# An attention and expert kernel with its first two experts' token lists cut in two parts each, six routing batches, and the routing of the last chunk put ahead

## The chip, the cores and the metric

One core of one Trainium2 chip runs the whole program. The metric is the device time of one execution in microseconds (us), taken as the median of several runs. A profiled execution gives the trace that the rows below come from.

## The reference

A decayed linear attention for 4 batches of 768 tokens with 8 heads of 64 features, and behind it a mixture of 16 experts (4 groups of 4), in which each of the 3072 tokens goes to one expert.

```python
for t in range(S):                      # attention, S = 768
    state = gamma * state + outer(k[:, :, t], v[:, :, t])
    y[:, :, t] = scale * (q[:, :, t] @ state)
x = y.transpose(0, 2, 1, 3).reshape(B * S, H * D)      # 3072 x 512
g_idx = argmax(x @ w_group, axis=1)                    # group, weight g_w by softmax
e_idx = argmax(xg @ w_expert[g], axis=1)               # expert in it, weight e_w by softmax
h = maximum(xg[mask_e] @ w1[g, e], 0)                  # 512 -> 1024
out[tok_idx] = (g_w * e_w)[:, None] * (h @ w2[g, e])   # 1024 -> 512
```

The inputs drawn with the reference's own seed give experts 0 and 1 (group 0) 210 and 200 tokens. Of expert 0's, 92 lie in the first 12 chunks of 128 tokens and 118 in the last 12; of expert 1's, 94 and 106.

## The kernel before, in words

**Attention** runs over 24 chunks of 128 tokens, six to a batch. For one chunk `attention` issues the products with the state (L262), with the scores of two chunks ago (L275), the new state (L238), a product that brings the logits of the chunk before into token order (L318), two groups of transposes (L195, L293), the scores of the chunk after next (L216) and the logits of this chunk (L307). VectorE multiplies the output by its decays (`xt`, L287) and masks the scores (`pf`, L223). All products that belong to routing write one PSUM tile, `log`.

**Routing** goes by batches of chunks (`BATCHES`). `route` is a generator of VectorE steps, one to a `yield`: logits to a one-hot matrix `oh`, the ranks of the tokens by a few small products of `oh` (L368, L370) into `log`, the softmax weights, then `r1` and `nb` (L397, L399), which read the ranks, and the token's slot (L419). `route_steps` draws a few steps at three places of each chunk. After the ranks' products it pauses for three calls. `enlist` then scatters each chunk's token numbers and weights into the experts' lists in DRAM (`meta`, L427, an indirect DMA that GpSimd issues), `listed` reads a list back (`mt`, L614, on SP's queue), `gather` fetches its tokens' rows (`xg`, L624, GpSimd), and `xtrans` transposes them and splits them into a 16-bit high and low part (L642 to L645).

**Experts.** Weights come as 1 MB loads (`wload`, L576; four to an expert, four buffers). `wsplit` cuts 512 or 1024 columns at a time into a high part on ScalarE (L601) and the rest on VectorE or GpSimd (L602). `layers` runs one tile of tokens: 96 products of the tile's width for the first layer (L665), ScalarE and VectorE making `hh` and `hl` from it (L670, L671), and a second layer of 24 products 512 wide (L689), or of 96 products of the tile's width where the tile has at most 116 tokens (L713, with transposes at L773). `scatter` writes the result (L792).

Experts 0 and 1 are done first, in tiles of their own, so that they can begin before the routing ends: `ua` (expert 0, up to 128 tokens of the first 12 chunks), `ub` (78 of the next 7), `uc` (59 of the rest), `va` (expert 1, 128 of the first 12 chunks), `vb` (128 of the rest). `order` then sorts the other 14 experts by their counts; `us[0]` to `us[13]` are run in that order with widths from 256 down to 173, each with the next one's loads and splits under it. Tokens that exceed a tile's width are left to a loop at the end (`general`).

The order on each engine is the order of the code: the schedule is manual, and each engine takes its instructions strictly in turn. Behind the last chunk the code emits, in this order: the rest of `ua`'s layers mixed with the last route, the scatters into the lists, the reads of `ub`'s list, `va`'s layers with the splits of `va`'s weights and the steps of `order` under them, `ub`, `uc`, `vb`, and `us[0]`. The loads of `us[0]`'s weights stand on GpSimd's queue, behind the gathers of `uc` and `vb`.

Of the kernel before, what the change touches and what calls it, by code (L numbers as in the profile page):

```python
# [13 lines left out]
U32 = mybir.dt.uint32  # L14
# [8 lines left out]
P = 128  # L23
# [36 lines left out]
BATCHES = [(0, 4), (4, 4), (8, 4), (12, 7), (19, 5)]  # L60
# [34 lines left out]
class Kernel:  # L95
    def __init__(self, tc, qk, vb, wr, w1p, w2p, cst, dec, out):
# [8 lines left out]
        self.pause = 0  # L105
# [220 lines left out]
    def route(self, i):  # L326
# [67 lines left out]

        rkv = rk.rearrange("p (c x) -> p c x", x=NX)
# [7 lines left out]
        V.tensor_tensor(r2, r1, oh[:, 0:n, :], ALU.mult)  # L403
        yield 1
# [10 lines left out]
        sf = t("sf")  # L415
        V.tensor_reduce(sf, r2, axis=AX.X, op=ALU.add)
        yield 1
        slot = rp.tile([P, BM], U32, name="slot", bufs=3)[:, 0:n]
        V.tensor_copy(slot, sf)  # L419
        yield 1  # L420
        self.todo += [(slot, src, c) for c in range(n)]

    def enlist(self, slot, src, c):
# [9 lines left out]
        if self.done > MIDDLE:  # L433
            tc.declare_no_dep(i.ins, group="middle", reason="no later token enters this list")
            tc.add_to_no_dep_group("middle", i.ins)
# [168 lines left out]
    def listed(self, u, group=None):  # L604
# [42 lines left out]
    def layers(self, u):  # L647
# [6 lines left out]
        for f2 in range(4):  # L654
# [16 lines left out]
            nc.vector.scalar_tensor_tensor(hl[:, f, 0:W], hv[:, :, 0:W], 0.0, hh[:, f, 0:W], ALU.max, ALU.subtract)  # L671
# [177 lines left out]
    def attention(self, extra, beside):  # L849
# [20 lines left out]
        for ch in range(NCH):  # L870
# [4 lines left out]
            steps = 4 if late else 5  # L875
# [14 lines left out]
            self.route_steps(steps)  # L890
# [262 lines left out]
```

## Time and profile before

| what | us |
|---|---|
| median of 3 runs (467.91 to 469.46) | 468.16 |
| the profiled execution | 468.46 |
| its span, from the first to the last instruction | 466.6 |
| PE busy in the span | 430.1 (92%) |
| DVE, ACT, POOL busy | 296.3, 235.1, 178.7 |

PE is TensorE's matmuls, PEld its weight loads, DVE VectorE, ACT ScalarE, POOL GpSimd, SPq and POOLq the queues on which DMAs are issued. An idle time stands in square brackets with what ended it. Starts of matmuls are true, while a busy time includes the pipeline's depth, so that steps are best taken from start to start. PEclk is the granted clock, 1.00 for 2.4 GHz.

### The profile page before, as it was taken

How to read it: one execution, taken by the hardware profiler on the slowest of the kernel's cores; microseconds unless marked ns; L12 is line 12 of the kernel's file. 1: busy time of each engine (PE TensorE's matmuls, PEld its weight loads, DVE VectorE, ACT ScalarE, POOL GpSimd, SP SyncE). 2: the span in 40 equal slices, each digit the busy share in tenths (PEclk: the TensorE clock that was granted, in tenths of full speed). 3: DMA queues.
4: the chain of work that ended last, by engine and by line, in shares of the span. 5: the costliest groups of instructions: out<-in, count | busy, mean ns of one | idle time of the engine just before them, and what ended most of it. 6: DMA issues, size and time to landing. Idle time of an engine off the chain costs nothing.

```text
span 466.6 us, 13547 instructions
## 1 busy us (share of the span) xinstructions
PE 430.1 (92%) x5679; PEld 348.5 (75%) x5679; DVE 296.3 (64%) x490; ACT 235.1 (50%) x398; POOL 178.7 (38%) x148
## 2 busy tenths in 40 slices
PE   7997989899789687799999999999999999999991
PEld 3886868788676287485878879788788788788770
DVE  2448476566549321867768897587777777787720
ACT  1333435444454033745556556665576676676610
POOL 3624557570585553210323335054153153142011
PEclk9999899999999798999999999999999999999997
DMA  7979797796560274676768687787977887987000
GB/s 244 353 235 313 233 266 229 254 287 208 179 222 2 53 295 181 217 256 235 247 211 243 244 251 256 275 269 270 291 263 271 305 274 271 325 278 286 11 29 30
DMA packets 36024, 106.86 MB, mean 229 GB/s; under 512 B 14687, under 2 KB 15327, under 8 KB 28283
## 3 DMA queue, kind: packets, MB, share of 16 engines
q1 hardware_dynamic: 24059, 88.65, 56.9%
q0 software_dynamic: 11904, 17.34, 10.7%
q8 instruction: 45, 0.74, 0.6%
q14 instruction: 16, 0.13, 0.1%
HBM read 93.55 MB, written 13.81 MB: 230 GB/s over the span
## 4 chain that ended last, share of the span: by engine, by line
PE 67%; issue 18%; POOL 6%; DVE 3%; DMA 2%; ACT 1%; SPq 1%; POOLq 0%; ACTq 0%
PE hps L665 21%; PE yps L739 8%; PE yps L689 7%; PE yps L741 5%; PE op L275 5%; PE sc L216 5%; PE op L262 2%; POOL out L792 2%; PE stp L238 2%; PE tpx L642 2%; PE tp L293 2%; PE kt L195 2%; PE log L307 2%; POOL meta L427 2%; POOL xg L624 1%
## 5 line engine op out<-in xcount | busy, mean ns | idle before, releaser
L602 DVE TENSOR_TENSOR wl<-wf,wh 128x1024 bf16<-128x1024 f32 (+1 forms) x121 | 144.6, 1204 | 39.8 <-ACT wh L601 39.6
L665 PE MATMUL hps<-xbl,wh 128*128 128x128 bf16 (+16 forms) x608 | 136.8, 243 | 2.9 <-DVE xbl L645 1.6
L665 PE MATMUL hps<-xbh,wh 128*128 128x128 f16 (+16 forms) x608 | 136.9, 243 | 2.2 <-ACT xbh L644 2.2
L665 PE MATMUL hps<-xbh,wl 128*128 128x128 f16 (+16 forms) x608 | 136.8, 243 | 0.0
L601 ACT ACTIVATE wh<-wf 128x1024 f16<-128x1024 f32 (+1 forms) x136 | 134.2, 999 | 0.1
L792 POOL DMA_INDIRECT out<-yo,mt x33 | 43.0, 1303 | 194.9 <-ACT yo L757 173.5
L665 PEld LDWEIGHTS <-wh 128*128 128x128 f16 x1216 | 105.2, 99 | 5.9 <-issue 3.3
L624 POOL DMA_INDIRECT xg<-xd,mt x33 | 53.3, 1614 | 26.7 <-DMA mt<-meta 13.3
L670 ACT ACTIVATE hh<-hps 128x256 f16<-128x256 f32 (+16 forms) x76 | 35.8, 472 | 54.4 <-PE hps L665 54.1
L665 PEld LDWEIGHTS <-wl 128*128 128x128 bf16 x608 | 59.7, 99 | 4.2 <-issue 3.3
L671 DVE SCALAR_TENSOR_TENSOR hl<-hps,hh 128x256 bf16<-128x256 f32 (+16 forms) x76 | 40.0, 528 | 35.9 <-ACT hh L670 35.5
L741 PEld LDWEIGHTS <-wh 128*128 128x128 f16 x704 | 44.7, 98 | 21.0
L223 DVE TENSOR_TENSOR pf<-sc,cst 128x512 f32<-128x512 f32 x48 | 30.9, 685 | 36.1 <-PE sc L216 36.1
L644 ACT ACTIVATE xbh<-tpx 128x512 f16<-128x512 f32 (+15 forms) x33 | 17.1, 517 | 49.9 <-PE tpx L642 49.8
L645 DVE TENSOR_TENSOR xbl<-tpx,xbh 128x512 bf16<-128x512 f32 (+15 forms) x33 | 19.4, 589 | 22.7 <-ACT xbh L644 22.6
L602 POOL TENSOR_TENSOR wl<-wf,wh 128x512 bf16<-128x512 f32 (+1 forms) x15 | 20.3, 1355 | 34.7 <-ACT wh L601 32.8
L739 PE MATMUL yps<-wh,hh 128*128 128x512 f16 x88 | 33.4, 380 | 0.0
L739 PE MATMUL yps<-wh,hl 128*128 128x512 f16 x88 | 33.4, 379 | 0.0
L739 PE MATMUL yps<-wl,hh 128*128 128x512 bf16 x88 | 33.4, 379 | 0.0
L427 POOL DMA_INDIRECT meta<-src,slot x24 | 27.4, 1140 | 9.5 <-issue 5.3
L741 PEld LDWEIGHTS <-wl 128*128 128x128 bf16 x352 | 23.1, 98 | 10.4
L216 PE MATMUL sc<-ld 64*128 64x128 f32 x384 | 28.4, 288 | 2.2 <-DMA ld<-qk 2.2
(138 smaller groups left out, 682.3 us busy)
## 6 DMA issues: line engine op xcount, KB each, us to landing
wf<-w1p SPq DMA_DIRECT2D x28, 1024.0 KB, 7.8
wf<-w2p SPq DMA_DIRECT2D x28, 1024.0 KB, 7.2
ld<-qk SPq DMA_DIRECT2D x23, 512.0 KB, 7.0
xd<-xr SPq DMA_DIRECT2D x24, 256.0 KB, 3.5
vt<-vb SPq DMA_DIRECT2D x6, 768.0 KB, 8.1
wf<-w1p SPq DMA_DIRECT2D x8, 256.0 KB, 4.3
wf<-w2p SPq DMA_DIRECT2D x8, 256.0 KB, 4.1
wf<-w1p POOLq DMA_DIRECT2D x2, 1024.0 KB, 7.0
```

The lines of the kernel that those rows point to most:

```text
L216: nc.tensor.matmul(s["sc", par][:, cs], kT[rs, cs], qT[rs, cs], start=True, stop=True)
L427: i = nc.gpsimd.indirect_dma_start(out=self.metaf, out_offset=bass.IndirectOffsetOnAxis(ap=slot[:, c:c + 1], axis=0), in_=src[:, c, :], in ...
L601: nc.scalar.activation(u["wh"][i][:, cs], u["wf"][i][:, cs], AF.Copy)
L602: (eng or nc.vector).tensor_tensor(u["wl"][i][:, cs], u["wf"][i][:, cs], u["wh"][i][:, cs], ALU.subtract)
L624: nc.gpsimd.indirect_dma_start(out=xg[0:r, i, :], out_offset=None, in_=self.xd[0:n, :], in_offset=bass.IndirectOffsetOnAxis(ap=mt[0:r, i, ...
L665: nc.tensor.matmul(hv[:, a, 0:W], l[:, k, fs], r[:, k, 0:W], start=(n == 0), stop=(n == 11))
L670: nc.scalar.activation(hh[:, f, 0:W], hv[:, :, 0:W], AF.Relu)
L671: nc.vector.scalar_tensor_tensor(hl[:, f, 0:W], hv[:, :, 0:W], 0.0, hh[:, f, 0:W], ALU.max, ALU.subtract)
L689: nc.tensor.matmul(ps[0:r, :], l[:, k, ts], m[k], start=(n == 0), stop=(n == 23))
L739: nc.tensor.matmul(big, h[:, k, 0:P], w[k], start=(n == 0), stop=(n == 23))
L741: nc.tensor.matmul(yv[:, d, 0:r], w[k][:, d * P:d * P + P], h[:, k, P:P + r], start=(n == 0 and d == 0), stop=(n == 23), skip_group_check= ...
L792: s = nc.gpsimd.indirect_dma_start(out=self.out, out_offset=bass.IndirectOffsetOnAxis(ap=mt[0:r, i, 0:1].bitcast(U32), axis=0), in_=yo[0:r ...
```

## The change

Expert 0 gets two tiles, `ua` and `ub`, both 128 wide, in place of 128, 78 and 59; `uc` is gone, and both experts' second tiles take all tokens after the 12th chunk. The batches of the route become 4, 4, 4, 5, 4 and 3 chunks. Within a batch the softmax weights come first and the ranks' products after them, with `r1` and `nb` right behind these, and only at the first place of a chunk. Six of expert 1's eight splits now stand in chunks 20 to 22 (two did before); the last four quarter splits of `ua` move from VectorE to GpSimd. Expert 1's loads come one in each of chunks 18 to 21. Behind the last chunk the route of the last batch is emitted at once, `hl` of the layers that run meanwhile is held back until its slots are made, and `order`, the loads of `us[0]` (now on SP's queue) and all gathers come ahead of `va`. The splits and loads of `us[0]` and `us[1]` begin under `ub` and `vb`.

```diff
-EARLY, MIDDLE = (12, 19)
-PARTS = [
-    [(EARLY, 128, 0), (MIDDLE, 78, NX), (NCH, 59, NX + 1)],
-    [(EARLY, 128, 1), (NCH, 128, NX + 2)],
-]
+EARLY = 12
+PARTS = [[(EARLY, P, e), (NCH, P, NX + e)] for e in range(2)]
...
-BATCHES = [(0, 4), (4, 4), (8, 4), (12, 7), (19, 5)]
+BATCHES = [(0, 4), (4, 4), (8, 4), (12, 5), (17, 4), (21, 3)]
...
                 if 4 <= ch <= 19:
-                    self.wsplit(ua, ch - 4, 16, nc.gpsimd if ch < 16 else nc.vector)
-                if ch in (18, 21, 22, 23):
-                    self.wload(va, (18, 21, 22, 23).index(ch))
-                if ch in (21, 22):
-                    self.wsplit(va, ch - 21, eng=nc.gpsimd)
+                    self.wsplit(ua, ch - 4, 16, nc.gpsimd)
+                if 18 <= ch <= 21:
+                    self.wload(va, ch - 18)
+                if ch in (20, 21):
+                    self.wsplit(va, 2 * ch - 40)
+                    self.wsplit(va, 2 * ch - 39, eng=nc.gpsimd)
...
                 if ch == NCH - 2:
+                    self.wsplit(va, 4)
+                    self.wsplit(va, 5)
                     self.first = self.layers(ua)
...
-                if ch == 20 and place == 1:
+                if ch == 19 and place == 1:
...
-            first(2)
+            first(1)
             self.logits(last)
+            assert not self.steps
+            route = self.route(len(BATCHES) - 1)
+            while next(route) != "wait":
+                pass
+            self.held = []
+            first(1)
             self.trans_mm(last)
             self.x_store(last)
             first(2)
...
+            for _ in route:
+                pass
             while self.todo:
                 self.enlist(*self.todo.pop(0))
-            self.gather(ub)
...
+            self.listed(ub)
+            self.listed(vb)
...
+            self.steps.append(self.order())
+            self.route_steps(99)
...
+            self.wsplit(va, 6)
+            self.wsplit(va, 7)
+            self.picked(us[0], 0)
+            self.listed(us[0])
+            for i in range(4):
+                self.wload(us[0], i)
...
-            self.picked(us[0], 0, (ET.SP, ET.Pool))
-            for i in range(4):
-                self.wload(us[0], i, nc.gpsimd)
...
-            for k in self.layers(uc):
...
```

The first place is PE in a chunk of the attention at whose start a batch's ranks are made (before, then after); `log` is the routing tile, and the last product of each piece writes it.

```order
L238 MATMUL stp<-vs,kk 64x64 x7
L368 LDWEIGHTS stri
L368 MATMUL log<-oh,stri 128x80 [waits Activation_49]
...
L370 MATMUL log<-oh,ones 128x16
L318 MATMUL log<-cst,ls 128x20
L293 MATMUL tp<-ident,xt 128x128 [waits PE_49]
...
L307 MATMUL log<-xt,wr 32x128 [waits DVE_49,Activation_49]
```

```order
L236 MATMUL stp<-vs,kk 64x64 x7
L387 LDWEIGHTS stri
L387 MATMUL log<-oh,stri 128x80 [waits Activation_49]
...
L389 MATMUL log<-oh,ones 128x16
L316 MATMUL log<-cst,ls 128x20 [waits DVE_49]
L291 MATMUL tp<-ident,xt 128x128 [waits PE_49]
...
L305 MATMUL log<-xt,wr 32x128 [waits Activation_49]
```

The wait on VectorE has moved from the last product of the chunk to the one right behind the ranks.

The second place is POOL from the last chunk's vector product on: before, five scatters into the lists behind a split, `ub`'s gather, a result, two gathers and the loads of `us[0]`; then after.

```order
L602 TENSOR_TENSOR wl<-wf,wh 128x1024 [waits DMAHW3_49,DMAHW0_49,DMAHW4_49,PE_49,Activation_49]
L427 DMA meta<-src,slot 60800x2 [waits DMASW6_49,DVE_49]
...
L427 DMA meta<-src,slot 60800x2 [waits DMASW2_49]
L624 DMA xg_80<-xd,mt 78x512 [waits DMAHW4_49,DMAHW6_49,DMAHW3_49,DMAHW7_49,DMAHW1_49,DMASW3_49]
L792 DMA out<-yo,mt 3072x512 [waits DMASW4_49,Activation_49]
L624 DMA xg_80<-xd,mt 59x512 [waits DMAHW4_49,DMAHW3_49,DMAHW5_49,DMAHW1_49,DMAHW7_49,DMASW5_49,PE_49]
...
L580 TENSOR_LOAD ord [waits DVE_49]
L576 ISA
L576 DMA wf<-w1p 128x2048 [waits DMASW0_49,Pool_49]
```

```order
L425 DMA meta<-src,slot 57600x2 [waits DMASW4_49,DVE_49]
...
L425 DMA meta<-src,slot 57600x2 [waits DMASW7_49]
L425 DMA meta<-src,slot 57600x2 [waits DMASW0_49,DVE_49]
L425 DMA meta<-src,slot 57600x2 [waits DMASW1_49]
L425 DMA meta<-src,slot 57600x2 [waits DMASW2_49]
L795 DMA out<-yo,mt 3072x512 [waits DMASW3_49,Activation_49]
L623 DMA xg_80<-xd,mt 128x512 [waits DMAHW5_49,DMAHW4_49,DMAHW6_49,DMAHW3_49,DMAHW7_49,DMAHW1_49,DMASW4_49]
L623 DMA xg_80<-xd,mt 128x512 [waits DMAHW7_49,DMASW5_49,PE_49]
```

Four scatters (of the batch of chunks 17 to 20) and three (of the last) now stand there, then `ua`'s result and the gathers; the loads are no longer on this queue.

The third place is VectorE behind the last batch's ranks, before and after.

```order
L419 CAST slot<-sf 128x5 [waits DVE_49]
L1034 MEMSET xg_2314 128x1024 [waits DMAHW3_49,DMAHW2_49,DMAHW6_49,DMAHW1_49,Pool_49]
L602 TENSOR_TENSOR wl<-wf,wh 128x1024 [waits DMAHW3_49,DMAHW5_49,DMAHW2_49,DMAHW6_49,DMAHW0_49,Activation_49]
...
L671 SCALAR_TENSOR_TENSOR hl<-hps,hh 128x2x128 [waits Activation_49] x3
...
L457 TENSOR_TENSOR gt<-key 1x256 [waits DVE_49]
...
L645 TENSOR_TENSOR xbl<-tpx,xbh 128x4x78 [waits Activation_49]
L476 CAST ord<-ordf 1x16 [waits DVE_49]
```

```order
L407 CAST slot<-sf 128x3 [waits DVE_49]
...
L1022 SCALAR_TENSOR_TENSOR hl<-hps,hh 128x2x128 [waits Activation_49] x2
L672 SCALAR_TENSOR_TENSOR hl<-hps,hh 128x2x128 [waits Activation_49]
L644 TENSOR_TENSOR xbl<-tpx,xbh 128x4x128 [waits Activation_49]
...
L475 CAST ord<-ordf 1x16 [waits DVE_49]
...
L601 TENSOR_TENSOR wl<-wf,wh 128x1024 [waits DMAHW2_49,Activation_49]
L601 TENSOR_TENSOR wl<-wf,wh 128x1024 [waits Activation_49]
```

The held `hl` come behind the slots, then `order`, and only two splits of expert 1 are left, behind `order`.

## Rows read from the trace of the kernel before

**Rows 1.** The profile page's first line.
```profile
span 466.6 us, 13547 instructions
```

**Rows 2.** Busy time by stretch of the span: us, then PE, PEld, DVE, ACT and POOL busy (with the number of instructions), granted clock, share of the DMA engines' time, GB/s.
```profile
140.00:150.00 10.00, 9.17 (x116) 7.04 (x116) 9.45 (x27) 4.40 (x7) 5.14 (x4) 1.00 0.02 2
150.00:160.00 10.00, 5.87 (x30) 2.82 (x28) 5.54 (x13) 0.82 (x2) 6.94 (x5) 0.80 0.12 35
170.00:180.00 10.00, 6.28 (x194) 6.07 (x191) 1.82 (x5) 2.78 (x7) 3.54 (x4) 1.00 0.99 391
230.00:250.00 20.00, 20.00 (x148) 15.06 (x146) 14.35 (x23) 11.13 (x15) 6.39 (x4) 1.00 0.71 240
```

**Rows 3.** What PE waited for in the first 135 us: us in total, times, longest.
```profile
PE log L307 <- DVE nb L399: 7.9, 4, 2.4
```

**Rows 4.** The timeline of chunks 6 to 8, PE and VectorE: start, us, engine, line, tile, shape, idle before.
```profile
45.28 0.43 PE L307 MATMUL log<-xt,wr 128*32 128x128 f32 x8 [2.43 <-DVE nb L399]
51.65 0.43 PE L307 MATMUL log<-xt,wr 128*32 128x128 f32 x8
52.01 0.67 PE L262 MATMUL op<-ld,V 64*64 64x128 f32 x16
53.31 0.86 DVE L287 TENSOR_TENSOR xt<-op,gx 128x256 f32<-128x256 f32 x2 [0.27 <-PE op L275]
54.09 0.40 PE L318 MATMUL log<-cst,ls 128*128 128x20 f32 x2
56.43 0.42 PE L307 MATMUL log<-xt,wr 128*32 128x128 f32 x8
```

**Rows 5.** The timeline in the last chunks: `ua`'s list and tokens, the start of chunks 22 and 23 (L262), and the start of `va` (the first 128-wide product at 144.89).
```profile
115.71 0.87 SPq L614 DMA_DIRECT2D mt<-meta  x2
118.33 1.09 POOL L624 DMA_INDIRECT xg<-xd,mt  x1 [13.33 <-DMA mt<-meta]
123.01 0.67 PE L262 MATMUL op<-ld,V 64*64 64x128 f32 x16
125.81 0.60 PE L642 MATMUL tpx<-ident,xg 128*128 128x128 f32 x4
129.30 0.67 PE L262 MATMUL op<-ld,V 64*64 64x128 f32 x16
144.89 0.22 PE L665 MATMUL hps<-xbh,wh 128*128 128x128 f16 x1
```

**Rows 6.** The timeline of the last route: VectorE's steps, the split on POOL beside one of them, and PE's wait for `oh`.
```profile
137.06 2.85 DVE L352 SCALAR_TENSOR_TENSOR q<-d,cst 128x100 f32<-128x100 f32 x1
137.63 2.15 POOL L602 TENSOR_TENSOR wl<-wf,wh 128x1024 bf16<-128x1024 f32 x1
140.83 0.20 PE L368 MATMUL log<-oh,stri 128*128 128x96 bf16 x1 [2.15 <-DVE oh L361]
143.50 0.17 DVE L419 CAST slot<-sf 128x5 uint32<-128x5 f32 x1
```

**Rows 7.** The timeline of the scatters into the lists on POOL (the fourth and fifth of five), the gather behind them, and SP's next reads of the lists.
```profile
149.36 2.58 POOL L427 DMA_INDIRECT meta<-src,slot  x1 [0.31 <-issue]
152.24 1.17 POOL L427 DMA_INDIRECT meta<-src,slot  x1 [0.30 <-issue]
153.71 1.08 POOL L624 DMA_INDIRECT xg<-xd,mt  x1 [0.30 <-issue]
154.58 10.80 SPq L614 DMA_DIRECT2D mt<-meta  x8
```

**Rows 8.** The chain of work that ended last, from the gather of `ub`'s tokens to `us[1]`: start, us, what. "issue" is time in which the engine waited for nothing that the profile shows.
```profile
157.14 0.78 PE tpx L642 x4
157.92 5.09 PE yps L689 x12
163.01 3.36 PE hps L665 x96
...
172.24 1.32 issue
...
177.59 2.98 issue
...
181.38 2.33 PE hps L665 x24
...
184.15 4.02 PE hps L665 x72
188.17 2.59 PE yps L689 x12
190.76 0.44 PE tpx L642 x4
...
197.37 11.99 PE hps L665 x95
...
220.56 10.08 PE hps L665 x96
```

**Rows 9.** Groups of instructions by line and shape: count, busy us, mean ns of one, idle before.
```profile
L601 ACT ACTIVATE wh<-wf 128x1024 f16<-128x1024 f32 x120 | 124.3, 1049 | 0.0
L602 POOL TENSOR_TENSOR wl<-wf,wh 128x1024 bf16<-128x1024 f32 x3 | 6.4, 2150 | 2.7 <-ACT wh L601 2.7
```

**Rows 10.** The page's DMA issues: count, KB of one, us from issue to landing.
```profile
wf<-w1p SPq DMA_DIRECT2D x28, 1024.0 KB, 7.8
```

More of the change, by code (lines that the diff above doesn't have):

```diff
@@ L393, in route @@
         yield 1
+        yield "wait"
+        rk = self.log[:, P:P + (n + 1) * NX]
+        nc.tensor.matmul(rk, self.stri, oh.rearrange("p c x -> p (c x)"), start=True, stop=False)
+        for k in range(1, n + 1):
+            nc.tensor.matmul(
+                rk[:, k * NX:], self.ones, oh[:, 0:n + 1 - k, :].rearrange("p c x -> p (c x)"),
+                start=False, stop=(k == n),
+            )
         rkv = rk.rearrange("p (c x) -> p c x", x=NX)
@@ L404, in route @@
         yield 1
+        sf = t("sf")
+        V.tensor_reduce(sf, r2, axis=AX.X, op=ALU.add)
+        yield 1
+        slot = rp.tile([P, BM], U32, name="slot", bufs=3)[:, 0:n]
+        V.tensor_copy(slot, sf)
+        self.todo += [(slot, src, c) for c in range(n)]
+        yield 1
         for e, parts in enumerate(PARTS):
@@ L432, in enlist @@
         tc.add_to_no_dep_group("meta", i.ins)
-        if self.done > MIDDLE:
-            tc.declare_no_dep(i.ins, group="middle", reason="no later token enters this list")
-            tc.add_to_no_dep_group("middle", i.ins)
+        if self.done > EARLY:
+            for group in ("early0", "early1"):
+                tc.declare_no_dep(i.ins, group=group, reason="no later token enters the first lists")
+                tc.add_to_no_dep_group(group, i.ins)
     def order(self):
@@ L615, in listed @@
             if group:
-                tc.declare_no_dep(d.ins, group=group, reason="no later token enters this list")
+                tc.declare_no_dep(d.ins, group=group, reason="no later token enters the first lists")
                 tc.add_to_no_dep_group(group, d.ins)
@@ L910, in attention @@
             self.route_steps(steps)
-            for _ in range(3 if late else 1):
+            for _ in range(4 if ch >= NCH - 2 else 2 if late else 1):
                 if self.todo:
@@ L917, in attention, with route_steps @@
             extra(ch)
-    def route_steps(self, n, calls=3):
-        if self.pause:
-            self.pause -= 1
+    def route_steps(self, n, ranks=False):
+        if self.waiting and not ranks:
             return
+        self.waiting = False
         for _ in range(n):
@@ L1043, in run @@
[L1043 removed]
+            self.wsplit(va, 6)
[4 more added lines that the diff above has]
+                self.wload(us[0], i)
+            pick(1)
+            self.listed(us[1])
+            for u, v in ((ub, ua), (vb, va)):
+                u["wh"], u["wl"] = v["wh"], v["wl"]
+            for k in self.first:
+                pass
+            self.gather(ub)
+            self.gather(vb)
```

118 lines of the change are left out of this document (35 added, 83 removed).

## The prediction

> **What bounds the kernel now.** The 14 other experts fill the second half: there PE is busy all the time at full clock (the last row of [rows 2]), and the change alters neither their products nor their order. So I looked for PE's idle time and for low clock ahead of them. There are two places. In the attention PE stands still four times, 7.9 us in all, until VectorE has read a batch's ranks [rows 3]. Between 140 and 200 us the stretches of 10 us show PE busy for 5.9 and 6.3 us in two of them and the clock at 0.80 in one [rows 2]. The timeline and the chain of waits then say what ends last there: the one-hot matrix of the last route, then `ub`'s tokens, then two stalls that the profile puts down to nothing [rows 6, 8]. The span is 466.6 us [rows 1], the execution 468.46 us, 0.30 us above the median; I make the sum against the execution and take 0.3 us off at the end.
>
> **The ranks in the attention.** One wait: the logits' product of chunk 6 came 2.43 us late and the next chunk took 51.65 - 45.28 = 6.37 us where the one after took 4.78 [rows 4]. So this first wait also cost 1.6 us of slow work. Now `r1` and `nb` follow the ranks' products at once, and what waits is the small product behind them. In chunk 8 `xt` ends at 54.17, 2.16 us after the chunk's start; `r1` and `nb` then take about 0.3 us and the wake-up 0.1 us, so that this product could go at 2.55 to 2.6; it stood at 54.09 - 52.01 = 2.08, and the ranks' own products add about 0.2 us [rows 4]. That leaves a wait of 0.3 us, five times, since the last batch's ranks lie behind the attention: -7.9 - 1.6 + 1.5 = **-8.0 us**. From above it is bounded by the old waits coming back, 5 x 2.0 in place of 7.9; from below by no wait at all, -9.5.
>
> **`ua`'s tokens.** Their list is read a chunk earlier, but on POOL the gather now stands behind a split of 2.15 us that itself waits for two ScalarE pieces of 1.05 us [rows 9]. These begin about 0.4 us into chunk 21, so the gather starts 0.4 + 2.1 + 2.15 + 0.3 = 4.95 us into it. From the gather of `ub` to the transposes behind it took 157.14 - 153.71 = 3.4 us [rows 7, 8]: the tokens are there 8.35 us into chunk 21, which is 3.6 us into chunk 22 if a chunk takes 4.8 us. PE asks for them at 125.81 - 123.01 = 2.8 us [rows 5]. **+0.8 us**; before, they had been there for long.
>
> **The last chunk and `ua`.** From chunk 23's start to `va`'s first product it took 144.89 - 129.30 = 15.6 us [rows 5], 2.15 of it the wait for `oh` [rows 6]. Now the logits' last step comes before a group of `ua`'s products and the VectorE steps run at once, with no split on POOL beside them; the ranks stand 24 products later. By my count of the order `oh` is there 6.4 us after the chunk's start and PE gets to the ranks at 6.9. The wait goes; an extra batch's ranks and their wait come in (0.3 + 0.4 us). 15.6 - 2.15 + 0.7 = 14.2: **-1.4 us**. The held `hl` are about three steps of 0.4 us behind the slots and done before the second layer asks for them.
>
> **`va`.** Before, from 144.89 to 163.01, 18.1 us [rows 5, 8]. A clean tile of 128 takes 96 products at 4.02/72 us, 5.36, and 24 at 2.59/12, 5.18, and transposes, 0.45 [rows 8]: 11.0 us. What goes is the wait for `ub`'s tokens, with 12 products at half speed behind it (5.09 us in place of 2.59 [rows 8]). Does a new wait take its place? Slots at about 8.4 us after chunk 23's start; four scatters of the batch before end at 8.9 and three more at 12.8 (1.0 us each plus 0.3 between them); SP reads the lists 154.58 - 153.41 = 1.2 us later [rows 7]; a gather starts 118.33 - 115.71 = 2.6 us behind that [rows 5], at 16.6, its tokens are there 3.4 us later, at 20.0. PE asks at 14.2 + 5.4 + 2.6 = 22.2. 2.2 us of slack, so **-7.1 us**. The cover is thin: the scatters took up to 2.58 us beside VectorE's splits [rows 7].
>
> **Expert 0's rest.** `ub` and `uc` took 181.38 - 163.01 = 18.4 us, 1.32 + 2.98 of it "issue" [rows 8]. One tile of 128 takes 11.0. **-7.4 us**. **`vb`**: 12.8 us from 181.38 to the end of `us[0]`'s transposes at 194.2; clean 11.4, with two groups of transposes: **-1.4 us**. The two stalls between `us[0]`'s transposes and its products stand in the same place in the new order, and so does its slow first layer (11.99 us, where a width of 245 takes 10.08 [rows 8]); I leave both.
>
> **What moves elsewhere.** `order`'s ten steps end at about 13.7 us after chunk 23's start, and SP can issue `us[0]`'s loads from then on, four within some 8 us; one lands in 7.8 us [rows 10]. The first split that needs them stands in the second layer of `ub`, at 33 us. Covered by 8 us; before, they waited behind two gathers on POOL. On SP they stand behind the reads of the lists, so `us[0]` is late if the scatters are. ScalarE's and VectorE's splits of `va` in chunks 20 to 22 are 2.1 and 1.2 to 2.4 us to a chunk, beside work of about 2.1 on each: under 4.8.
>
> The sum: -8.0 + 0.8 - 1.4 - 7.1 - 7.4 - 1.4 = **-24.5 us**.
>
> **Costs that no row gives.** (a) The gather of `ub` late: from 0 to the old 4.1 us with 2.5 us of slow clock; I take 0.5, by the slack. (b) Stalls like the two "issue" gaps: they lay where the DMA engines were 99% busy [rows 2] with four loads at once and PE was at its shortest products (59 wide); now the loads come while products of 128 run, at half as many to a microsecond. 0 to 4.3 us; I take 0.5. (c) VectorE's steps beside POOL's splits: one step took 2.85 us beside a split of 2.15, and ended when it did [rows 6]. Two such splits now stand in chunks 21 and 22, 0 to 4.3 us; VectorE has slack there, and I take 1.0. No gain is possible, as the edit only adds work there. (d) `us[0]` at full clock from the start, -1.7 to 0; I take 0. Together +2.0, so 468.46 - 22.5 - 0.3 = **445.7 us**.
>
> On (c), the Trainium skill ("SBUF — State Buffer", section "Who interferes with whom") has a VectorE instruction with two SBUF inputs and a GpSimd instruction that reads SBUF lock each other out for the whole instruction. The row of 2.85 us agrees. It speaks against laying a split on each engine side by side, as chunks 20 and 21 now do; by it the worst would be one split length for each pair, no more than the bound above.
>
> **The rivals.**
> 1. *The gather of `ub` is late*: the new wait takes the old one's place. For: seven scatters stand ahead of it, and a result of `ua`; four of them could not start earlier. Against: nothing but three VectorE steps and `order` runs beside them, and the splits that stretched them come later. 445.7 + 6.6 - 0.5 = 451.8.
> 2. *The splits stretch chunks 20 to 23*: POOL has about 9.8 us of work in chunk 20 (two scatters, splits of 1.2 and 2.15, two gathers, one scaling) against 4.8, and `ua`'s tokens come 3 us later still; with (c) whole, 445.7 + 3 + 3.3 = 452.
> 3. *The rank wait only moves*: the product behind the ranks waits about as long as the logits' product did, 2.0 us five times in place of 0.3, since VectorE is behind. Then the change doesn't do what its ranks were moved for; 445.7 + 8.5 = 454.2. Against: nothing stands between `xt` and `r1` in VectorE's new order.
> 4. *All clean*: (a) to (c) nothing, `us[0]` fast: 468.16 - 24.5 - 1.7 = 442.0.
> 5. *Slower*: the clock falls to its 1.2 GHz level at the wait for `ua`'s tokens and stays there until `us[0]`, 48 us of work; at half speed throughout that is +48, near 490. It turns the sign once 22.5 of these 48 us are spent twice. For: the low clock behind the wait of 4.1 us. Against: behind the waits of 1.7 to 2.15 us in the last chunks the clock was 1.00 (the first row of [rows 2]), and PE has no longer gaps to come.
>
> That tokens spill into the loop at the end is ruled out: the second lists hold 118 and 106 of 128.
>
> **How the numbers follow.** Forecast 0.60; rivals 1 to 5: 0.12, 0.10, 0.06, 0.07, 0.02. That is 0.97, of which 0.95 is faster by far more than the 0.3%, 1.4 us, that a measurement of this kernel can tell from no change. The 0.03 left are for what I don't see in an order that no run has shown: 0.02 no change, 0.01 slower, 0.03 slower with rival 5. The range takes rival 4 less the last of the rank waits, 441, up to rival 2 with some of (b), 453.
>
> **What would show it.** PE's waits on `nb` near 1.5 us in all at the product behind the ranks; one wait under 1 us at `ua`'s transposes; none for `oh`; `ub`'s transposes without a wait and the second half of `va`'s second layer at 2.6 us; no gap at "issue"; `us[0]`'s first layer some 22 us earlier. I am wrong if POOL or VectorE, not PE, sets the pace from chunk 20 to `va`, or if `us[0]`'s weights come late.

## The result, and the profile after

The changed kernel takes 455.16 us (median of 4 runs, 453.38 to 458.14) where the kernel before takes 468.81 beside it: a ratio of 0.9715 (0.9658 to 0.9772). It is faster, as forecast, but by 13.6 us and not by 22.5: 9.5 us above the predicted 445.7 and 2.2 above the top of the range.

The page's first line of the changed kernel, to set beside [rows 1]:

```profile
span 453.3 us, 12946 instructions
```

To find where the missing time went, both traces are cut at the same places of the program. Each number is the distance between two starts read from the timeline or the chain of waits, in us. A chunk starts with its first value product (L275 before, L273 after), a tile with its first product. The column "predicted" is the prediction's sum without its 2.0 us of unknown costs. Four runs, told below, stand in the last columns; e5 is the changed kernel once more.

| stretch | before | predicted | after | e5 | e12 | e9 | e10 |
|---|---|---|---|---|---|---|---|
| start to chunk 5 | 34.2 | 34.2 | 35.9 | 36.3 | 34.4 | 33.9 | 34.4 |
| chunks 5 to 21 | 82.3 | 88.5 for this and the next | 81.3 | 81.4 | 77.8 | 79.2 | 72.9 |
| chunks 21 to 23 | 13.4 | | 17.0 | 15.7 | 17.7 | 13.3 | 13.9 |
| chunk 23 to `va` | 15.0 | 13.6 | 13.6 | 15.7 | 14.0 | 13.2 | 13.3 |
| `va` | 18.1 | 11.0 | 13.1 | 16.6 | 15.3 | 11.1 | 11.1 |
| expert 0's rest | 18.4 | 11.0 | 11.0 | 11.0 | 11.0 | 11.0 | 11.0 |
| `vb` to `us[1]` | 39.2 | 37.8 | 36.3 | 38.0 | 38.0 | 38.0 | 38.0 |
| `us[1]` to the end | 246.0 | 246.0 | 245.1 | 245.0 | 244.9 | 245.3 | 245.1 |

Behind the attention two terms hold to the tenth (the last chunk and expert 0's rest), `va` is 2.1 us longer than predicted, and `vb` to `us[1]` is 1.5 us shorter. The same program spreads there: e5 has 3.5 us more in `va` and 2.1 more ahead of it. The miss is in the attention: chunks 5 to 23 take 98.3 us where 88.5 were predicted, even more than the 95.7 before.

What PE waited for in the first 205 us of the changed kernel (total, times, longest), the view of [rows 3]:

```profile
PE tpx L641 <- DMA xg<-xd,mt: 5.2, 2, 3.4
PE log L305 <- DVE xt L285: 4.8, 5, 1.3
...
PE log L316 <- DVE nb L397: 2.6, 5, 0.7
...
PE log L316 <- ACT ls L310: 0.9, 2, 0.6
```

The waits of 7.9 us on `nb` are 2.6 now; but 4.8 us on `xt`, 0.9 on `ls` and 5.2 on two gathers have come. The timeline shows where they come from, first at the first batch's ranks, to set beside [rows 4], then in chunk 22, beside [rows 5] (start, us, engine, line, tile, shape, idle before):

```profile
37.91 1.16 POOL L601 TENSOR_TENSOR wl<-wf,wh 128x512 bf16<-128x512 f32 x1 [8.63 <-ACT wh L600]
38.12 0.98 DVE L371 TENSOR_TENSOR eg<-sm,o 128x16 f32<-128x16 f32 x1
39.03 1.04 POOL L169 TENSOR_TENSOR vs<-vt,cst 128x512 f32<-128x512 f32 x1
39.22 0.87 DVE L377 TENSOR_SCALAR u<-sm 128x4 f32<-128x4 f32 x1
40.01 0.74 DVE L285 TENSOR_TENSOR xt<-op,gx 128x256 f32<-128x256 f32 x2
40.57 0.65 PE L305 MATMUL log<-xt,wr 128*32 128x128 f32 x8 [0.79 <-DVE xt L285]
...
43.41 0.40 PE L316 MATMUL log<-cst,ls 128*128 128x20 f32 x2 [0.47 <-DVE nb L397]
...
121.42 1.06 POOL L623 DMA_INDIRECT xg<-xd,mt  x1 [0.15 <-issue]
...
125.79 2.52 DVE L377 TENSOR_SCALAR u<-sm 128x4 f32<-128x4 f32 x1
126.14 2.13 POOL L601 TENSOR_TENSOR wl<-wf,wh 128x1024 bf16<-128x1024 f32 x1
127.94 1.12 PE L641 MATMUL tpx<-ident,xg 128*128 128x128 f32 x4 [3.44 <-DMA xg<-xd,mt]
128.63 1.21 DVE L601 TENSOR_TENSOR wl<-wf,wh 128x1024 bf16<-128x1024 f32 x1
129.76 0.75 DVE L285 TENSOR_TENSOR xt<-op,gx 128x256 f32<-128x256 f32 x2
130.32 0.88 PE L305 MATMUL log<-xt,wr 128*32 128x128 f32 x8 [1.26 <-DVE xt L285]
```

Two softmax steps of a few numbers each take 0.98 and 0.87 us, and each ends just behind an instruction of GpSimd's. They now stand ahead of `xt`, so `xt` comes late and the logits' product with it. In chunk 22 one such step takes 2.52 us, a split of 1.21 follows it, and `ua`'s tokens land 6.5 us after their gather's start, not 3.4.

From the chain of waits, what [rows 8] showed before:

```profile
150.40 7.22 DMA xg<-xd,mt
...
160.90 5.36 PE hps L664 x96
...
171.89 5.36 PE hps L664 x96
...
186.44 10.53 PE hps L664 x95
...
208.18 10.08 PE hps L664 x96
```

Expert 0's rest is 171.89 - 160.90 = 11.0 us, without a gap. `ub`'s gather was issued when predicted (16.8 us after chunk 23's start, counted as in the prediction from the product with the state; predicted 16.6), but took 7.2 us to land; the four loads of `us[0]` were issued from 150.45 on, right behind it.

### The profile page after: what moved, and what is told of

It reads as the page before. It is cut to its first block, busy times and chain, and to the rows that moved or that the text cites. A ratio compares the mean times of both kernels' runs of the same rounds, so it can differ in the third digit from the quotient of the medians.

```text
span 453.3 us, 12946 instructions
## 1 busy us (share of the span) xinstructions
PE 421.5 (93%) x5373; PEld 340.8 (75%) x5404; DVE 298.4 (66%) x498; ACT 232.7 (51%) x391; POOL 173.1 (38%) x145
## 4 chain that ended last, share of the span: by engine, by line
PE 67%; issue 12%; DVE 7%; DMA 5%; POOL 4%; ACT 1%; SPq 1%; POOLq 0%; DVEq 0%; ACTq 0%
PE hps L664 24%; PE yps L742 10%; PE yps L744 7%; PE yps L692 7%; PE sc L214 4%; PE op L273 3%; PE tpx L641 2%; POOL out L795 2%; DMA xg<-xd,mt 2%; DMA meta<-src,slot 2%; PE log L305 1%; PE op L260 1%; PE stp L236 1%; PE kt L193 1%; PE tp L291 1%
## 5 line engine op out<-in xcount | busy, mean ns | idle before, releaser
L601 DVE TENSOR_TENSOR wl<-wf,wh 128x1024 bf16<-128x1024 f32 x118 | 143.0, 1220 | 44.9 <-ACT wh L600 44.8
L664 PE MATMUL hps<-xbh,wh 128*128 128x128 f16 (+14 forms) x576 | 135.1, 246 | 1.8 <-ACT xbh L643 1.8
L664 PE MATMUL hps<-xbl,wh 128*128 128x128 bf16 (+14 forms) x576 | 135.1, 246 | 1.1 <-DVE xbl L644 1.1
L664 PE MATMUL hps<-xbh,wl 128*128 128x128 f16 (+14 forms) x576 | 135.0, 246 | 0.0
L669 ACT ACTIVATE hh<-hps 128x256 f16<-128x256 f32 (+14 forms) x72 | 35.1, 488 | 55.1 <-PE hps L664 54.8
L672 DVE SCALAR_TENSOR_TENSOR hl<-hps,hh 128x256 bf16<-128x256 f32 (+14 forms) x70 | 38.6, 551 | 18.6 <-ACT hh L669 18.2
L643 ACT ACTIVATE xbh<-tpx 128x512 f16<-128x512 f32 (+13 forms) x32 | 16.9, 527 | 50.1 <-PE tpx L641 50.0
L644 DVE TENSOR_TENSOR xbl<-tpx,xbh 128x512 bf16<-128x512 f32 (+13 forms) x32 | 19.2, 601 | 21.4 <-ACT xbh L643 21.3
L425 POOL DMA_INDIRECT meta<-src,slot x24 | 24.1, 1004 | 19.6 <-DVE oh L343 8.8
L169 POOL TENSOR_TENSOR vs<-vt,cst 128x512 f32<-128x512 f32 x24 | 25.2, 1050 | 14.6 <-DMA vt<-vb 14.6
```

Of the source, the lines that this page charges most:

```text
L601: (eng or nc.vector).tensor_tensor(u["wl"][i][:, cs], u["wf"][i][:, cs], u["wh"][i][:, cs], ALU.subtract)
L664: nc.tensor.matmul(hv[:, a, 0:W], l[:, k, fs], r[:, k, 0:W], start=(n == 0), stop=(n == 11))
L669: nc.scalar.activation(hh[:, f, 0:W], hv[:, :, 0:W], AF.Relu)
L672: nc.vector.scalar_tensor_tensor(*rest)
```

## The experiments

Three theories. **1, the tokens**: `ua`'s late gather stops chunk 22, and most hangs on that. **2, GpSimd on VectorE**: GpSimd's splits stretch VectorE's small steps, and VectorE's queue ahead of `xt` becomes the bound. **3, the rank wait only moved**: the softmax steps were put ahead of `xt`, whatever GpSimd does.

The kernels ran on four chips, each group beside the kernel before; that took 474.5 us beside e1 to e4, 474.1 beside e5 to e8, 465.5 beside e9 to e11 and 468.1 beside e12. So ratios to it are compared, not times; even these have to be taken with care from one group to another, since the kernel before spread by up to 1.5% within a group.

| run | us | ratio to before (95%) |
|---|---|---|
| e1, gather first | 458.72 | 0.9682 (0.9622 to 0.9743) |
| e2, splits on VectorE | 460.40 | 0.9708 (0.9647 to 0.9769) |
| e3, softmax behind `xt` | 459.42 | 0.9687 (0.9640 to 0.9734) |
| e4, before with two tiles | 472.52 | 0.9959 (0.9921 to 0.9996) |
| e5, the changed kernel again | 460.04 | 0.9684 (0.9621 to 0.9746) |
| e6, VectorE cleared | 454.75 | 0.9602 (0.9559 to 0.9645) |
| e7, loads on GpSimd's queue | 460.29 | 0.9710 (0.9666 to 0.9755) |
| e8, both | 451.09 | 0.9523 (0.9480 to 0.9567) |
| e9, ranks behind the logits | 447.45 | 0.9601 (0.9556 to 0.9645) |
| e10, all of `ua`'s splits off GpSimd | 441.46 | 0.9462 (0.9418 to 0.9505) |
| e11, before with ranks at once | 464.02 | 0.9954 (0.9921 to 0.9986) |
| e12, changed kernel, `ua`'s splits on VectorE | 452.80 | 0.9702 (0.9597 to 0.9806) |

### e1, e2, e3: one suspect each

e1 moves the gather ahead of the split in chunk 20:

```diff
+                if ch == 20:
+                    self.gather(ua)
                 if ch in (20, 21):
...
                 if ch == 20:
-                    self.gather(ua)
                     self.gather(va)
```

> The changed kernel, with the gather of expert 0's first tokens (`ua`) put ahead of chunk 20's split on GpSimd instead of behind it; expert 1's gather stays. Theory 1 (the tokens were late, and most of what was missed hangs on that): the gather goes at about 117.8 us instead of 121.42; with the 6.5 us that it took to land it is there at 124.3, just before TensorE asks, so the wait of 3.44 us at the transposes goes, and with it the late `xt` behind it (1.26 us) and part of the slow clock: 455.2 - 4 to 6 = 449 to 451. Theory 2 (the splits on GpSimd stretch VectorE's steps in chunks 20 to 22): the wait at the transposes goes, but `xt` of chunk 22 stays late behind a stretched softmax step: 452 to 453. Theory 3 (the rank wait only moved to `xt` and `nb`, everywhere): 454 or more, with the waits of chunks 6 to 18 as they are.

e2 takes the two splits from GpSimd:

```diff
-                    self.wsplit(va, 2 * ch - 39, eng=nc.gpsimd)
+                    self.wsplit(va, 2 * ch - 39)
```

> The changed kernel, with expert 1's two splits on GpSimd in chunks 20 and 21 moved to VectorE. The gathers, which stood behind the first of them, then go early too. Theory 1: the gain is that of the early gather alone, the same as when only the gather is moved, to within 1 us. Theory 2: on top of it the two stretched softmax steps (1.51 and 2.52 us, 0.24 and 0.16 us elsewhere) come back to their usual size, `xt` of chunk 22 is in time, and the time is 1 to 3 us below that of the moved gather alone. Against both: VectorE gets 2.4 us of splits more, 1.2 us to a chunk; if that is what bounds these chunks, the time is that of the changed kernel or above.

e3 draws fewer steps ahead of `xt`:

```diff
-            self.route_steps(steps, True)
+            self.route_steps(7, True)
...
-            self.route_steps(steps)
+            self.route_steps(3)
```

(the last at both later places of a chunk).

> The changed kernel, with three of a batch's routing steps drawn at the second and third place of a chunk instead of five or six, so that the one-hot steps stay ahead of `xt` and the softmax steps come behind it on VectorE; the ranks' products stay in their places. Theory 3: the waits of the logits' product on `xt` (0.77, 0.77, 0.77 and 1.19 us in chunks 6, 10, 14 and 19 or so) go, and the waits on `nb` and `ls` shrink or stay: 455.2 - 2.5 to 4 = 451 to 452.7. Theories 1 and 2: these small waits cost nothing more than what they show, -1 to -3.5, and the 3.44 us at the transposes of chunk 22 stay.

None of the three is told from the changed kernel by its ratio (0.9715, and 0.9684 in e5, which ran on another chip). The traces say why. In e1 the wait for the tokens is gone and chunks 21 to 23 take 14.6 us in place of 17.0, but `xt` is late by 1.71 us. In e2 no step of chunk 22 is stretched, yet both splits now stand on VectorE ahead of `xt`, and the logits' product waits 2.81 us. In e3 the tokens come in time as well, though nothing was done for them, and the wait on `xt` is 4.12 us. Timeline of e3, then of e2, in chunk 22:

```profile
123.73 0.60 PE L641 MATMUL tpx<-ident,xg 128*128 128x128 f32 x4
123.83 2.74 DVE L356 TENSOR_TENSOR o<-q,m 128x80 f32<-128x80 f32 x1
124.34 2.13 POOL L601 TENSOR_TENSOR wl<-wf,wh 128x1024 bf16<-128x1024 f32 x1
126.75 1.22 DVE L601 TENSOR_TENSOR wl<-wf,wh 128x1024 bf16<-128x1024 f32 x1
127.89 0.75 DVE L285 TENSOR_TENSOR xt<-op,gx 128x256 f32<-128x256 f32 x2
128.45 0.65 PE L305 MATMUL log<-xt,wr 128*32 128x128 f32 x8 [4.12 <-DVE xt L285]
```

```profile
126.00 0.16 DVE L377 TENSOR_SCALAR u<-sm 128x4 f32<-128x4 f32 x1
126.49 2.35 DVE L601 TENSOR_TENSOR wl<-wf,wh 128x1024 bf16<-128x1024 f32 x2
128.75 0.75 DVE L285 TENSOR_TENSOR xt<-op,gx 128x256 f32<-128x256 f32 x2
129.31 0.65 PE L305 MATMUL log<-xt,wr 128*32 128x128 f32 x8 [2.81 <-DVE xt L285]
```

So theory 1 falls as a whole: take the late tokens away, and VectorE's queue ahead of `xt` stops the same product. e5, the changed kernel itself (told below), says so without any edit: there the tokens were in time too, at most 5.0 us after the same gather, and `xt` stopped the product 1.77 us long:

```profile
122.04 1.06 POOL L623 DMA_INDIRECT xg<-xd,mt  x1 [0.15 <-issue]
...
127.06 0.60 PE L641 MATMUL tpx<-ident,xg 128*128 128x128 f32 x4
...
129.43 0.65 PE L305 MATMUL log<-xt,wr 128*32 128x128 f32 x8 [1.77 <-DVE xt L285]
```

Chunks 21 to 23 take 15.7 us there. Against that e1's 14.6 is a gain of 1.1 us and not of 2.3: the rest came without e1's edit. Theory 3 is worth 1.9 us in chunks 5 to 21 (79.4 us in e3; chunks 21 to 23 then take 18.5, so that nothing of it reaches the end), less than the 2.5 expected: with the softmax behind `xt`, GpSimd's instructions stretch a one-hot step there instead (2.18 us for `d` in chunk 9).

### e4 and e11: one part of the change in the old kernel

```diff
-PARTS = [
-    [(EARLY, 128, 0), (MIDDLE, 78, NX), (NCH, 59, NX + 1)],
-    [(EARLY, 128, 1), (NCH, 128, NX + 2)],
-]
+PARTS = [[(EARLY, P, e), (NCH, P, NX + e)] for e in range(2)]
...
```

> The kernel before, with one part of the change alone: expert 0 in two tiles of 128 instead of 128, 78 and 59, the list of the second read behind all scatters; route, splits, loads and gathers as before. By the prediction's term the rest of expert 0 is 7.4 us shorter, 4.3 us of it the two stalls at products 59 wide. Against it, the second tile's list is now read only behind the last scatter, so that its gather starts about 1.2 + 2.6 us later and TensorE waits that much more: 468.8 - 7.4 + 3.8 = 465.2. If the two stalls stay (they come from the loads of the next weights on GpSimd's queue, not from the 59-wide products): 469 to 470. If the tile change needs no other part: 461.4.

Expert 0's rest takes 11.0 us here, -7.4 as predicted, and the stalls of 1.32 and 2.98 us are gone with the narrow tiles (two of 0.15 and 0.31 stand in `vb`). The wait for `ub`'s tokens is 3.08 us. The time falls by 0.4%; the 0.8% forecast (0.992) lies just inside the interval. In this profile chunks 5 to 21, whose code is that of before, took 91.0 us, 9 us longer than in the profile of before, with a granted clock of 0.91 where that had 0.98. The kernel before was itself 5.7 us slower on this chip than in the first pair, and no profile of it was kept there, so whether the edit has a part in it isn't shown. One place of it is the strongest case of theory 2: GpSimd ran three scalings in a row, and a split on VectorE waited for all three:

```profile
103.10 4.24 DVE L596 TENSOR_TENSOR wl<-wf,wh 128x512 bf16<-128x512 f32 x1 [0.98 <-ACT wh L595]
103.73 3.05 POOL L168 TENSOR_TENSOR vs<-vt,cst 128x512 f32<-128x512 f32 x3
```

e11 puts the softmax ahead of the ranks and reads these at once, in the old kernel:

```diff
+        ex = t("ex", 5, 4)
...
         yield "wait"
         rk = self.log[:, P:P + (n + 1) * NX]
...
-            self.route_steps(steps)
+            self.route_steps(steps, True)
```

> The kernel before, with one part of the change alone: softmax ahead of the ranks, and the ranks read at once, at the first place of a chunk; batches 4, 4, 4, 7 and 5, tiles, splits and gathers as before. By the prediction's first term the four waits of 7.9 us and their slow work of 1.6 go and four waits of 0.3 come: -8.3 us, 460 on the first pair's scale, ratio 0.982. By what the changed kernel's profile shows (each batch costs 1.8 to 2.3 us in all, waits on `xt`, `ls` and `nb` together, where it had cost 2.4 to 5 before): -2 to -4 us, ratio 0.991 to 0.996.

0.9954 (0.9921 to 0.9986) is -2.1 us: the second alternative. By time the prediction's largest term, -8.0, brings a quarter alone. The trace gives it a little more: chunks 5 to 23 take 91.9 us, 3.8 less than in the profile of before, while start to chunk 5 took 2.2 us more. The waits on `nb` fall from 7.9 to 1.9 us, and 2.8 us on `xt` and 0.8 on `ls` are there instead.

### e5 to e8: both stops at once

e5 is the changed kernel itself.

> The changed kernel itself, once more, beside its variants: the yardstick for them. In its first profile TensorE had no gap at "issue" behind the attention; in the profiles of its three variants there were five to eight such gaps of 0.2 to 0.5 us in `va`'s first layer, beside the loads of `us[0]`. If they belong to the variants, this run has none and a ratio as before, 0.9715; if they come and go with the run, it has them and is some 2 us above.

It has the gaps. They lie in the second half of `va`'s first layer (the first and the last of seven, 2.7 us in all):

```profile
153.11 0.22 PE L664 MATMUL hps<-xbh,wh 128*128 128x128 f16 x1 [0.15 <-issue]
...
157.49 0.22 PE L664 MATMUL hps<-xbl,wh 128*128 128x128 bf16 x1 [0.51 <-issue]
```

So the gaps don't belong to the variants: the same program has none in its first profile. Whether the chip or the run decides isn't shown; e6 and e8, on e5's chip, have none in this layer. The 2 us that were expected on top are not there as a ratio (0.9684 against 0.9715).

e6 takes `ua`'s gather and the softmax as e1 and e3 do, and lays the rest halves of expert 1's splits behind `xt`:

```diff
+            beside(ch, 2)
...
-                    self.wsplit(va, 2 * ch - 40)
+                    self.wsplit(va, 0, later=True)
...
+                if place == 2 and ch in (21, 23):
+                    self.rest()
```

> The changed kernel, with three things at once: `ua`'s gather ahead of chunk 20's split, the softmax steps behind `xt`, and the rest halves of expert 1's splits of chunks 20 to 23 taken out of the way of `xt` on VectorE: one stays on GpSimd, the others come right behind `xt` of chunks 21 and 23, behind `ua`'s tokens in chunk 22, and in `va`'s first layer. Theory 2, in the form that the three variants leave (chunks 22 and 23 are bound by VectorE's queue ahead of `xt`; the late tokens only hide it): both stops in chunk 22 go, the two chunks take 4.8 to 5.5 and 6.3 to 7 us in place of 4.8 and 12.2, so -4.5 to -6; with the softmax steps' 1.9 us, 447 to 450 by the first pair's scale (ratio 0.955 to 0.962). Theory 1 (the tokens): no more than moving the gather alone and the softmax alone add up to, 2 to 4 us. Against both: later splits press on `va`'s second layer; if that waits for them, nothing is gained in all.

e7 undoes one part of the change:

```diff
-            self.picked(us[0], 0)
+            self.picked(us[0], 0, (ET.SP, ET.Pool))
...
+            for i in range(4):
+                self.wload(us[0], i, nc.gpsimd)
```

> The changed kernel, with one part undone: the loads of `us[0]`'s weights stand on GpSimd's queue behind the gathers, as before the change, instead of on SP's. If the loads are what made `ub`'s gather slow (7.2 us to land, TensorE waiting 1.8 us) and what goes with the gaps at "issue" in `va`'s first layer: the wait goes, the gaps move later or go, -1.8 us or more. If the gather is slow by itself: no change of it, and the loads come 4 us later, which nothing feels, since the first split of `us[0]` stands in `ub`'s second layer.

e8 is e6 with e7's edit.

> The two versions above together: VectorE cleared ahead of `xt`, and the loads of `us[0]` behind the gathers on GpSimd's queue. If their gains lie in different stretches (the attention's last chunks; `va`), they add up: 2 to 4 us below the better of the two, some 444 to 447 by the first pair's scale (ratio 0.947 to 0.955).

e6 gains (0.9602), within its expected band, but not by the way that was expected. Chunk 22's stop is still there: chunks 21 and 22 take 5.8 and 9.6 us, not 4.8 to 5.5 and 6.3 to 7, with 1.44 us of wait on `xt`, 1.04 on `xbl` and a granted clock of 0.83 in chunk 22. Beside e5's profile e6 is 0.3 us shorter in chunks 21 to 23, 2.8 in chunks 5 to 21 and 2.1 ahead of chunk 5, where nothing was changed; so, as far as one profile of each can tell, the band was met in part by luck. e7 gains nothing that can be told. There TensorE had the gaps in `va`, as in e5, and came too late to feel the gather. Five of the seven gaps lie ahead of the loads, which start at 156.19 in e7: the loads don't make these, and e7 alone says nothing of the gather. e6 and e8 do: without the gaps and differing in that one edit, they show the gather beside the loads, then ahead of them:

```profile
146.09 0.91 SPq L576 DMA_DIRECT2D wf<-w1p  x2
146.12 1.23 POOL L631 DMA_INDIRECT xg<-xd,mt  x1 [0.30 <-issue]
...
154.31 0.66 PE L649 MATMUL tpx<-ident,xg 128*128 128x128 f32 x4 [3.74 <-DMA xg<-xd,mt]
```

```profile
147.24 1.23 POOL L631 DMA_INDIRECT xg<-xd,mt  x1 [0.30 <-issue]
...
151.47 0.60 PE L649 MATMUL tpx<-ident,xg 128*128 128x128 f32 x4
...
152.68 1.18 POOL L576 DMA_DIRECT2D wf<-w1p  x2
```

Beside the loads the tokens are there 8.2 us after the gather's start; ahead of them, within 4.2, and `va` takes the 11.0 us that were predicted. e8 stands at 0.9523, 3.7 us below e6: within the 2 to 4 us expected.

### e9, e10, e12: the batches' own cost

e9 is e8 with the ranks' products behind the transposes of their chunk:

```diff
-            self.route_steps(7, True)
...
                 self.x_store(ch - 1)
                 del self.st[ch - 1]["xt"]
+                self.route_steps(7, True)
```

> The best version so far (VectorE cleared ahead of `xt`, loads behind the gathers; ratio 0.9523), with the ranks' products moved behind the small logits' product and the transposes of their chunk, so that `r1` and `nb` run while TensorE does the scores. There each batch still cost 1.4 to 1.9 us: about 0.5 us of wait on `nb` at the small product (1.0 in the first batch) and up to 1.3 us on `xt` a chunk earlier. If the wait on `nb` is only a matter of what TensorE does next on the routing tile: the 2.9 us of it go, -2 to -2.9 us, ratio 0.946 to 0.948. If it moves again (to the ranks' products, which then wait for ScalarE's copy of the small product's result): no change.

e10 is e9 with `ua`'s splits behind `xt` on VectorE:

```diff
-                    self.wsplit(ua, ch - 4, 16, nc.gpsimd)
+                    self.wsplit(ua, ch - 4, 16, later=True)
```

> The version with the ranks behind the logits, and in addition the 16 quarter splits of `ua` (chunks 4 to 19) taken from GpSimd to VectorE, one right behind `xt` of each chunk. If GpSimd's instructions are what stretches VectorE's small steps (0.9 to 2.2 us in place of 0.2, each ending just behind an instruction of GpSimd's), fewer of them are stretched, the wait on `xt` in a batch's first chunk shrinks from 0.6 to 1.3 us to about 0.3, and the time falls by 1 to 2.5 us. If VectorE's load is what counts: 0.6 us more of it in each of 16 chunks, behind `xt` where it idles 1.2 to 2.4 us, and nothing or a loss of 1 us.

In e9 the waits on `nb` fall from 2.9 us to 0.5, but little of it is left: a wait on `xt` grew to 1.99 us in one batch, and chunks 5 to 21 take 79.2 us where e8 took 79.5. The ratio, on another chip, shows no gain either (0.9601 against 0.9523). On the same chip e10 takes 441.46 us against e9's 447.45, all of it in chunks 5 to 21 (72.9 against 79.2), and more than the 1 to 2.5 us expected. Some 3.4 us of that are waits on `xt`; some of the rest is the clock, 0.91 between 53 and 73 us in e9, behind the wait of 1.99 us, and 1.00 in e10. Timeline of e9 at that batch, then of e10:

```profile
54.27 1.01 POOL L426 DMA_INDIRECT meta<-src,slot  x1 [0.17 <-PE op L274]
54.33 0.24 DVE L348 TENSOR_TENSOR d<-L,m 128x80 f32<-128x80 f32 x1
54.60 2.98 DVE L351 SCALAR_TENSOR_TENSOR q<-d,cst 128x80 f32<-128x80 f32 x1
55.31 1.18 POOL L606 TENSOR_TENSOR wl<-wf,wh 128x512 bf16<-128x512 f32 x1
56.42 1.05 POOL L170 TENSOR_TENSOR vs<-vt,cst 128x512 f32<-128x512 f32 x1
...
58.30 0.75 DVE L286 TENSOR_TENSOR xt<-op,gx 128x256 f32<-128x256 f32 x2
58.87 0.65 PE L306 MATMUL log<-xt,wr 128*32 128x128 f32 x8 [1.99 <-DVE xt L286]
```

```profile
53.57 0.24 DVE L351 SCALAR_TENSOR_TENSOR q<-d,cst 128x80 f32<-128x80 f32 x1
...
54.54 0.75 DVE L286 TENSOR_TENSOR xt<-op,gx 128x256 f32<-128x256 f32 x2
```

The same step takes 2.98 us beside a row of GpSimd's work and 0.24 without it. In e10 no wait on `xt` or `nb` of 0.2 us or more is left in chunks 6 to 21. VectorE got the splits' work on top and the kernel was faster all the same, so VectorE's load was not what counted. That is theory 2.

The Trainium skill ("SBUF — State Buffer", "Who interferes with whom") lets the one of VectorE and GpSimd that issues first hold the shared pair of ports for the whole instruction. The rows agree that a step ends when GpSimd's work does, but 2.98 us is longer than any one instruction there: the waiting step got in only when a split and a scaling, 2.16 us together, were both over. Ahead of them stood a scatter's issue; as `d` ran its 0.24 us beside the start of that, its part is not certain. The bound that the prediction drew from the section, one split length to a pair, was too low.

e12 makes that one move in the changed kernel itself:

```diff
-                    self.wsplit(ua, ch - 4, 16, nc.gpsimd)
+                    self.wsplit(ua, ch - 4, 16)
```

> The changed kernel, with one word changed: `ua`'s 16 quarter splits (chunks 4 to 19) run on VectorE instead of GpSimd, in their old place; all the rest as changed, expert 1's two splits on GpSimd in chunks 20 and 21 too. In the version with VectorE cleared, the same move took 6 us and all waits on `xt` of chunks 6 to 19 away, and the steps that GpSimd's row of split and scaling had stretched to 2.2 and 3.0 us took 0.24. If that stretching is what the prediction missed in chunks 6 to 20, the waits on `xt` (0.8 to 1.2 us, four of them) shrink to 0.3 or less here too, those on `nb` (0.5) and the stops of chunks 22 and 23 stay: -2.5 to -4 us, ratio 0.960 to 0.963 where the changed kernel has 0.968 to 0.972. If the splits, now ahead of `xt` in every chunk, load VectorE too much: 0.967 or above.

The ratio, 0.9702, is not the 0.960 to 0.963 expected, and its interval is too wide to tell it from the changed kernel. In its trace chunks 5 to 21 take 77.8 us in place of 81.3 and 81.4 (e5), -3.5 as expected, and one wait on `xt` is left of four:

```profile
100.69 0.65 PE L305 MATMUL log<-xt,wr 128*32 128x128 f32 x8 [0.37 <-DVE xt L285]
```

But the stops of chunk 22 remain, `ub`'s tokens are 2.23 us late, and between 150 and 160 us, around these tokens, the granted clock is 0.83, part of it at 1.2 GHz, where the changed kernel's first profile had 1.00, 2.4 GHz all along (stretch, us, busy PE, PEld, DVE, ACT, POOL, clock, DMA share, GB/s; e12 first, then the changed kernel):

```profile
150.00:160.00 10.00, 7.77 (x44) 3.77 (x43) 0.99 (x2) 1.28 (x2) 1.16 (x2) 0.83 1.01 417
```

```profile
150.00:160.00 10.00, 8.15 (x83) 5.55 (x82) 2.67 (x6) 1.75 (x4) 4.19 (x5) 1.00 0.91 350
```

`va` takes 15.3 us against 13.1, and `us[0]`'s first layer 12.20 against 10.53: 3.9 us, more than was won before. That is not e12's doing: in e5 the changed kernel itself takes 16.6 and 12.20 us there. So the trace shows that the cause is removed in chunks 5 to 21, and the time, in four runs, does not show the gain.

## Why the prediction was wrong

**The ranks in the attention, -8.0.** This is the step that failed. The wait on `nb` did become small (0.47 us four times and 0.70 once, predicted 0.3), and the slow work behind the old waits went (granted clock in chunks 5 to 21: 0.98 before, 1.00 after). But I costed the two instructions behind the ranks and took the softmax steps, which the change moved ahead of `xt`, at nothing. My point against rival 3, that nothing stands between `xt` and `r1`, looked at the wrong side of `xt`. With the waits on `xt` (3.5 us in chunks 5 to 19, of which 0.6 was there before) and `ls` (0.9) and 0.7 more on `nb` than taken, 4.5 us came back there; the table's chunks 5 to 21 miss 5.3 (before 82.3; of the 9.5 taken off, 2.0, the last wait, lies at the end of chunk 21; plus four waits of 0.3: 76.0; measured 81.3), and the other 0.8 no wait explains. e12 and e10 show the cause: VectorE's small steps beside GpSimd's. With `ua`'s splits taken from GpSimd, and the softmax still ahead of `xt`, 3.5 of the 5.3 us are gone.

**`ua`'s tokens +0.8, and the splits' 1.0 (cost c).** Mis-sized together: chunks 21 to 23 take 17.0 us where 12.5 follow from the terms, 13.5 with cost (c). The gather began 4.8 us into chunk 21 (predicted 4.95), but landed in 6.5 us, with the DMA engines 93% busy; I had taken 3.4 from a gather beside which they were 31% busy. Beside it one step took 2.52 us. In e5 the tokens were in time, and the stretch took 15.7 us. e1, e2, e3 and e5 show that these stops lie side by side, so that taking one away uncovers the next; e8's 13.9, which still has 1.32 us of wait on `xt`, is the shortest with the ranks in their place.

**`va`, -7.1.** Mis-sized by 2.1: rival 1's wait came, 1.80 us, not from the scatters, which ended in time for the gather, but from the loads beside the gather (e6 against e8).

**The last chunk -1.4, expert 0's rest -7.4, `vb` -1.4** hold: 13.6, 11.0, and `vb` with `us[0]` 1.5 us better than forecast, as `us[0]`'s first layer ran in 10.53 us in this profile. That is luck: I had taken 0 for cost (d), and the layer takes 10.53 us in e6 too, but 12.2 in e5, e8, e9, e10 and e12. The granted clock goes with it, 1.00 over the layer in the first profile and in e6, 0.87 in e8, e9 and e12; on what the clock hangs no experiment says. The 13.6 us of the last chunk are not firm either: e5 has 15.7, with gaps of 0.41 and 1.18 us at "issue" in it.

**Start to chunk 5, +1.7**: in the code nothing differs there; 0.9 us of it are longer waits for the first loads (`ld`, 3.1 us against 2.2). Over the profiles this stretch took 33.9 to 36.4 us, 34.2 in e6 and 34.4 in e12, so it belongs to the run or the chip.

**The rivals.** I gave 1, 2 and 3 a price and a chance each, as if one alone could come. All three came in part: 2 us, some 4.5 and 5, and the third at another product than the one I had named. They have the same root, queues that I had filled further, and should have been one case with a chance of its own.

## What to carry over

Before a step is moved "into VectorE's slack", look at what GpSimd runs at that place: beside a row of its instructions a step of 0.2 us can take 3, so that the slack ahead of the product that waits must cover the row, not the step. A landing time read while the queues are nearly idle is a lower bound; take one from beside loads of the size that will run there. Where several queues meet at one product, undo all suspects together first: one by one (e1, e2, e3) they gave nothing that can be told, while e8 takes 451.09 us beside e5's 460.04 on the same chip, and taking `ua`'s splits off GpSimd as well brings another 6 us (e10 against e9). And profile the changed kernel twice before reading its waits: the wait of 3.44 us at `ua`'s tokens, the largest of the first profile, was not there in the second.

## What was not expected of the hardware

A VectorE instruction waits behind several GpSimd instructions in a row, 2.98 us for a step of 0.24, and 4.24 for a split of 0.69, with three scalings of 3.05 us beside it.

A gather's landing went with the share of the DMA engines' time that was in use meanwhile: 3.4 us at 0.31 to 0.35 (before, e4), at most 4.2 at 0.54 (e8), at most 5.0 at 0.65 (e5, e7), 6.1 to 8.2 at 0.80 to 0.98 (e10, e9, the changed kernel, e12, e6). One gather doesn't fit: `uc`'s 59 rows in e11 took 8.2 us at 0.40, and were 5.8 us under way before the next expert's loads were issued. Why is open.

And the same program had seven gaps at "issue" in `va`'s first layer in one profile and none in another; in e7 five of them lie ahead of the loads, so the loads are not needed for them, and what their cause is stays open.
